# Tap weights through TensorE, one row group of taps and the negated sines on GpSimd, ssm_k first in the queue

## The chip, the core and the metric

The kernel runs on one core of one Trainium2 chip. A core has TensorE (matmuls, into PSUM), VectorE, ScalarE, GpSimd and SyncE, each with its own instruction queue; SyncE and ScalarE also issue loads and stores. The metric is the device time of one execution in microseconds, taken as the median of several runs. The profile calls TensorE PE, its weight loads PEld, VectorE DVE, ScalarE ACT, GpSimd POOL and SyncE SP; a "q" behind a name means the queue that issues, not the engine's own work. L12 is line 12 of the kernel.

## The reference

A block with a long convolution, computed by Fourier transforms, followed by a two-layer network. S is 2048 positions, D is 512 channels. Cut to what matters here:

```python
k_shift = sum(k_pad[:, t:t + S, :] * shift_k[:, ks - 1 - t] for t in range(4))   # four taps a channel
kv = k_shift * v
y = irfft(rfft(pad(kv)) * rfft(pad(ssm_k)))[:S] + kv * ssm_D
h = x + layernorm(x) * y
out = h + relu(layernorm(h) @ w1) @ w2
```

`shift_k` is 512x4 (the tap weights), `ssm_k` 512x2048, `ssm_D` 512; all in bf16.

## The kernel before

The Fourier transforms are done as matmuls with tables of sines in several stages. The whole program is written out in one order by hand; each engine works through its own queue strictly in that order, and semaphores hold it where another engine's result is not there yet.

**Loads at the start.** SyncE's queue issues, in this order: `wsh`, the tap weights as 128 partitions x 4 row groups x 4 taps, which are runs of four bf16 numbers, eight bytes each (L123); `sk`, the 2 MB of ssm_k (L124); then for four chunks `c` of 512 positions the transposed load of k into `kT[c]` (L134, L136) and of v into `vT` (L137). ScalarE's queue issues two small loads of ssm_D (L128). The 512 channels are four "row groups" of 128.

**Zero products.** Until ssm_k has landed, TensorE multiplies zeros: `fill(ps, n)` issues n matmuls of 128x512 whose result nobody reads, 28 at L158.

**Small tables.** GpSimd makes index ramps, the two unit matrices `identw` and `ident` (L178), the large ramp `r2` (L180) and the mask `dmask` (L246). VectorE makes `wf`, the tap weights in float32 (L191), and the angles `t1`, `t3` (helper `_turns`, L44 and L46), the parts `f1hi` and `f1lo` of the first stage's table (L215), and the large angles `tsn` (L222, L220). ScalarE makes sixteen diagonal matrices `wdiag`, `ident` times one column of `wf` each (L204).

**Transposes.** `to_rows` turns ssm_k by 32 matmuls with `identw` (L284) into five PSUM tiles `pst`, which ScalarE (L287) and VectorE (L289) copy out.

**The loop over `gb`, seven groups.** In each group `taps(c, h)` does two row groups of one chunk: four matmuls of 128x512 per row group with `wdiag` (one per tap, L335), and then VectorE multiplies the sum by v in place (L338). So chunk 1, row groups 2 and 3 are done in group 3. Then `stage1` does 32 small matmuls (L300) into two PSUM tiles `ps1`; VectorE adds the mask and copies one half of each (L312), ScalarE copies the other half of each (L315). The copies of one tile wait for each other: ScalarE's second copy comes after VectorE's first, and VectorE's second after ScalarE's first.

**The PSUM ring.** `bank2` hands out four tiles of two banks in a ring. A tile can be written again once the readers of the tile four places earlier are done. A group of the loop takes three: one `pkv` for the taps and two `ps1` for stage1. So the first `ps1` of a group waits for the L338 of the group before, and the second `ps1` for both copies out of the first `ps1` of the group before.

**Sines in the loop.** `st` holds three blocks of 64 columns per row: the sines of `tsn` (one big instruction before the loop, L236), the sines of `r2`, and the negated sines of `tsn`. `more_sines(gb)` behind group gb makes one half of a block on ScalarE (L236): in groups 0 and 1 the negated ones, in groups 2 and 3 those of `r2`. Behind group 1 `ec_turns(0)` lets GpSimd write new angles over the first half of `tsn` (L257, L260), which therefore has to wait until the negated sines have read it. Behind group 3 VectorE wraps these angles (`ec_wrap`, L264), and ScalarE makes four sines of them (`ec_sins`, L268), one behind each of groups 4 and 5 and two inside group 6.

**Then.** GpSimd makes tables for later (L362 to L370) and, once the last of the four sines has been read from the memory that they share, the sum tables `smc` (L377, L383), which the first sums (L459) read at 50.8 us. Behind the loop `vT` is turned (L284), stage1 of group 7 and eight groups of stage1 of `xfl` follow (evictions L273, L275), then the products in the frequency domain, the inverse stages (L584, L675) and the network (L687, L703). None of these is touched.

Of the kernel before, what the change touches and what calls it, by code (L numbers as in the profile page):

```python
# [9 lines left out]
ALU = mybir.AluOpType  # L10
BF16 = mybir.dt.bfloat16
F32 = mybir.dt.float32  # L12
# [3 lines left out]
P = 128  # L16
# [25 lines left out]
def _turns(nc, out, r, col, M, quarter):  # L42

    nc.vector.tensor_scalar(out=out, in0=r, scalar1=col, scalar2=float(M // 2 + (M // 4 if quarter else 0)),  # L44
                            op0=ALU.mult, op1=ALU.add)
    nc.vector.tensor_single_scalar(out=out, in_=out, scalar=M - 1, op=ALU.bitwise_and)  # L46
# [10 lines left out]
def kernel(  # L57
# [13 lines left out]
    nc = tc.nc  # L71
    _, S, D = A_q.shape
    DFF = B_w1.shape[1]
    KS = A_shift_k.shape[1]
    assert S == 2048 and D == 512 and KS == 4, "kernel is specialised to S=2048, D=512, ks=4"
    NT = 16
    DC = D // P
# [7 lines left out]
    consts = pl.push("consts")  # L85
# [5 lines left out]
    early = pl.push("early", side="right")  # L91
# [8 lines left out]
    G = turnp.tile([P, 4096], I32, name="G")  # L100
    taken = [15424]

    def view(at, n, dt, t=E):
        return t[:, at:at + n].bitcast(dt)

    def small(shape, dt):
        n = math.prod(shape) * (2 if dt == BF16 else 4) // 4
        v = view(taken[0], n, dt)
        taken[0] += n
        return v.rearrange("p (a b) -> p a b", a=shape[0]) if len(shape) == 2 else v  # L110

    CH = 512
    sk = view(0, 4096, BF16).rearrange("p (c t) -> p c t", c=DC)
    kfl = view(4096, 4096, BF16).rearrange("p (c n) -> p c n", c=P)
    vT = view(8192, 4096, BF16).rearrange("p (c t) -> p c t", c=DC)
    wdiag = view(12288, 1024, BF16).rearrange("p (r j c) -> p r j c", r=DC, j=KS)
    kT = [view(13312 + 1056 * c, 1056, BF16).rearrange("p (r t) -> p r t", r=DC) for c in range(2)]
    kT += [view(1056 * c, 1056, BF16, F).rearrange("p (r t) -> p r t", r=DC) for c in range(2)]
    r2 = G[:, 0:2048].rearrange("p (a b) -> p a b", a=32)
    tsn = G[:, 2048:4096].rearrange("p (a b) -> p a b", a=32)  # L120

    wsh = consts.tile([P, DC, KS], BF16, name="wsh")
    nc.sync.dma_start(out=wsh[:], in_=A_shift_k.rearrange("(r p) j -> p r j", p=P))  # L123
    nc.sync.dma_start(out=sk, in_=A_ssm_k.rearrange("(c p) t -> p c t", p=P))  # L124
    draw = small([DC * P], BF16)
    for dp in range(2):
        src = bass.AP(tensor=A_ssm_D.tensor, offset=A_ssm_D.offset, ap=[[0, 1], [1, DC * P]])
# [22 lines left out]
    def bank2(name):  # L150
        return psum.tile([P, 2, 512], F32, tag="ps", name=name)[:]

    def fill(ps, n):

        for _ in range(n):
            nc.tensor.matmul(out=ps, lhsT=zero[:], rhs=zero[:].unsqueeze(1).to_broadcast([P, 4, P]), start=True, stop=True, skip_group_check=True)

    fill(bank2("psz")[:, 0, :], 28)  # L158

    n1i = early.tile([P, 1], I32, name="n1i")  # L160
    for s in range(0, P, 32):
# [12 lines left out]
    ident = early.tile([P, P], BF16, name="ident")  # L174
    identw = early.tile([P, P], F32, name="identw")
    for t in (identw, ident):
        nc.gpsimd.memset(t[:], 0.0)
        nc.gpsimd.affine_select(out=t[:], in_=t[:], compare_op=ALU.not_equal, fill=1.0,  # L178
                                base=0, pattern=[[-1, P]], channel_multiplier=1)
    nc.gpsimd.iota(r2, pattern=[[2, 32], [128, 64]], base=1, channel_multiplier=0)  # L180
    pi4 = consts.tile([P, 2], I32, name="pi4")
    nc.gpsimd.iota(pi4[:], pattern=[[0, 2]], base=0, channel_multiplier=1)
# [4 lines left out]
    n2c = consts.tile([P, 1], F32, name="n2c")  # L187
    nc.vector.tensor_copy(out=n1c[:], in_=n1i[:])
    nc.vector.tensor_copy(out=n2c[:], in_=n2i[:])
    wf = early.tile([P, DC, KS], F32, name="wf")  # L190
    nc.vector.tensor_copy(out=wf[:], in_=wsh[:])  # L191
    t1 = small([64], I32)
    _turns(nc, t1[:, 0:32], r1[:], n1c[:], 128, True)
    _turns(nc, t1[:, 32:64], r1[:], n1c[:], 128, False)
    t3 = small([2, 64], I32)
    _turns(nc, t3[:, 0, :], r3[:], n2c[:], 64, True)
    _turns(nc, t3[:, 1, :], r3[:], n2c[:], 64, False)
# [19 lines left out]
    st = stp.tile([P, 32, 192], F32R, name="st")  # L217
# [17 lines left out]
    def big_sin(out, turns, scale):  # L235
        nc.scalar.activation(out=out, in_=turns, func=ACT.Sin, scale=scale * TURN / 8192)  # L236
# [18 lines left out]
    def ec_turns(q):  # L255
        w = ecw[q]
        nc.gpsimd.iota(w[:, 1, :].rearrange("p (i a n) -> p i a n", i=4, a=4), pattern=[[1, 4], [16, 4], [64, 32]],  # L257
                       base=4 * q, channel_multiplier=0)
        for h, off in ((0, 4096 + 2048), (1, 0)):
            nc.gpsimd.tensor_scalar(out=w[:, h, :], in0=w[:, 1, :], scalar1=k1o[:], scalar2=float(off),  # L260
                                    op0=ALU.mult, op1=ALU.add)

    def ec_wrap(q):
        nc.vector.tensor_single_scalar(out=ecw[q], in_=ecw[q], scalar=8191, op=ALU.bitwise_and)  # L264

    def ec_sins(q, rs=range(DC)):
        for r in rs:
            nc.scalar.activation(out=ecore[q][:, :, :, r // 2, r % 2, :], in_=ecw[q].rearrange("p h (i x) -> p h i x", i=4),  # L268
                                 func=ACT.Sin, scale=esc[:, r:r + 1], bias=ebi[:, r:r + 1])
# [22 lines left out]
    def stage1(fl, B, gb, dmul=None):  # L292

        j, sp = gb // 2, gb % 2
        pss = [bank2("ps1").rearrange("p b (a w r l x) -> p (b a) (w r) l x", a=2, w=2, r=2, l=2) for _ in range(2)]
        for gi in range(8):
            g = 16 * j + 4 * (gi // 2) + 2 * sp + gi % 2
            for f, first in ((f1hi, True), (f1lo, False)):
                for rp, rows in enumerate(halves):
                    nc.tensor.matmul(out=pss[rp][:, gi // 2, :, gi % 2, :],  # L300
                                     lhsT=fl[rows, 2 * g:2 * g + 2, :].rearrange("p d n -> p (d n)"),
                                     rhs=f[rows].rearrange("p w r v h -> p (w r v h)"), start=first, stop=not first,
                                     tile_position=(64 * rp, 0), skip_group_check=True)
        o = [B.rearrange("p i (u w) (v s) x -> p i u w v s x", w=2, s=2)[:, :, 4 * j:4 * j + 4, :, :, sp, 4 * rp:4 * rp + 4]
             .rearrange("p i u w v x -> p i (u w) v x") for rp in range(2)]
        pv = [p.rearrange("p u (w r) l (v i) -> p i (u w) v (r l)", w=2, i=2) for p in pss]
        if dmul is None:
            for rp in range(2):
                copy("AD"[rp], o[rp], pv[rp])
            return  # L310
        for rp in range(2):
            nc.vector.tensor_tensor(out=o[rp][:, 0], in0=pv[rp][:, 0],  # L312
                                    in1=dmul[:, rp, sp, 4 * j:4 * j + 4].rearrange("p u w x -> p (u w) x").unsqueeze(2)
                                    .to_broadcast([P, 8, 16, 4]), op=ALU.add)
            nc.scalar.copy(out=o[1 - rp][:, 1], in_=pv[1 - rp][:, 1])  # L315
# [4 lines left out]
    big_sin(st[:, :, 0:64], tsn, 1)  # L320

    def more_sines(i):
        half = slice(16 * (i % 2), 16 * (i % 2) + 16)
        if i < 2:
            big_sin(st[:, half, 128:192], tsn[:, half], -1)
        else:
            big_sin(st[:, half, 64:128], r2[:, half], 1)

    def taps(c, h, each=2):

        for r0 in range(2 * h, 2 * h + 2, each):
            ps = bank2("pkv")[:, 0:each, :]
            for i in range(each):
                for j in range(KS):
                    nc.tensor.matmul(out=ps[:, i, :], lhsT=wdiag[:, r0 + i, j, :],  # L335
                                     rhs=kT[c][:, r0 + i, 16 - j:CH + 16 - j], start=(j == 0), stop=(j == KS - 1))
            vv = vT[:, r0:r0 + each, CH * c:CH * c + CH]
            nc.vector.tensor_tensor(out=vv, in0=ps, in1=vv, op=ALU.mult)  # L338
# [2 lines left out]
    inv3 = consts.tile([P, 2, 2, 64], F32R, name="inv3")  # L341
    inv12 = consts.tile([P, 2, 64], F32R, name="inv12")
    ones = consts.tile([P, P], F32R, name="ones")

    for gb in range(7):
        if gb < 6:
            taps(gb // 2, gb % 2)
        else:
            taps(3, 0)
            taps(3, 1, 1)  # L350
            ec_sins(0, (2, 3))
        stage1(kfl, BK, gb, dmask)
        if gb < 4:
            more_sines(gb)
        if gb == 1:
            ec_turns(0)
        if gb == 3:
            ec_wrap(0)
        if gb in (4, 5):
            ec_sins(0, (gb - 4,))  # L360

    nc.gpsimd.memset(inv3[:].bitcast(F32), 0.0)  # L362
    nc.gpsimd.tensor_tensor(out=dpm[:, 0, :], in0=dsc[:, 0, :], in1=dsc[:, 1, :], op=ALU.add)
# [118 lines left out]
    for c in range(8):  # L482
        units, early = {}, {}
# [43 lines left out]
    st = late.tile([P, 4, 6], F32, name="st")  # L527
# [185 lines left out]
    psz = pl.push("psZ", space=PSUM)  # L713
# [74 lines left out]
```

## Time and profile before

| what | us |
|---|---|
| median of three runs (207.43 to 208.14) | 207.6 |
| the profiled execution | 207.31 |
| its span, first to last instruction | 205.2 |
| TensorE busy | 197.6 |
| VectorE busy | 141.9 |
| ScalarE busy | 116.4 |
| GpSimd busy | 69.4 |

An engine's busy time is the union of its instructions' spans. In a timeline a row gives start, length, engine, line, operation, output<-input with sizes, and how many instructions of one kind are merged in it (x8); in square brackets stands how long the engine sat idle before it and what released it. In the chain of waits, each piece is what the end of the program had to wait for at that moment, with its start and length. A table by stage gives for each stretch its length and then the busy time of PE, PEld, DVE, ACT and POOL with the number of instructions, the granted TensorE clock, the busy share of the DMA engines, and GB/s.

### The profile page before, as it was taken

How to read it: one execution, taken by the hardware profiler on the slowest of the kernel's cores; microseconds unless marked ns; L12 is line 12 of the kernel's file. 1: busy time of each engine (PE TensorE's matmuls, PEld its weight loads, DVE VectorE, ACT ScalarE, POOL GpSimd, SP SyncE). 2: the span in 40 equal slices, each digit the busy share in tenths (PEclk: the TensorE clock that was granted, in tenths of full speed). 3: DMA queues.
4: the chain of work that ended last, by engine and by line, in shares of the span. 5: the costliest groups of instructions: out<-in, count | busy, mean ns of one | idle time of the engine just before them, and what ended most of it. 6: DMA issues, size and time to landing. Idle time of an engine off the chain costs nothing.

```text
span 205.2 us, 4606 instructions
## 1 busy us (share of the span) xinstructions
PE 197.6 (96%) x1869; PEld 138.1 (67%) x1869; DVE 141.9 (69%) x246; ACT 116.4 (57%) x190; POOL 69.4 (34%) x118
## 2 busy tenths in 40 slices
PE   8999999988999999999999999999999999999991
PEld 2475555977899999899998844475444844444460
DVE  5989898699789998997652875998098642360130
ACT  5776779788577877677781088304940164026200
POOL 7962800991467996122003032052102200002000
PEclk9999999999999999999999999999999999999997
DMA  5999980001700000064526999899806805310011
GB/s 151 345 214 196 199 141 3 0 5 16 265 0 3 0 3 3 0 130 78 102 67 194 208 221 144 169 154 136 120 16 126 140 25 52 84 58 13 0 51 51
DMA packets 47819, 19.93 MB, mean 97 GB/s; under 512 B 42710, under 2 KB 46264, under 8 KB 47800
## 3 DMA queue, kind: packets, MB, share of 16 engines
q1 hardware_dynamic: 44144, 16.15, 41.6%
q10 hardware_dynamic: 3656, 3.51, 6.3%
q8 instruction: 14, 0.23, 0.5%
q14 instruction: 5, 0.04, 0.1%
HBM read 7.02 MB, written 2.10 MB: 44 GB/s over the span
## 4 chain that ended last, share of the span: by engine, by line
PE 90%; DMA 4%; ACT 2%; DVE 1%; issue 1%; SPq 0%
PE ps1m L687 19%; PE ps2m L703 19%; PE psi L584 11%; PE us L459 8%; PE ps L300 8%; PE pz L675 7%; PE u L437 7%; PE pkv L335 7%; DMA E<-in_A_ssm_k_dram 4%; PE pst L284 3%; PE pm L507 1%; ACT xfl L287 0%; ACT BX L273 0%; DVE BX L475 0%; DVE BK L312 0%
## 5 line engine op out<-in xcount | busy, mean ns | idle before, releaser
L689 ACT ACTIVATE M<-ps1m 128x512 bf16<-128x512 f32 (+1 forms) x44 | 25.1, 595 | 49.4 <-PE ps1m L687 39.0
L703 PE MATMUL ps2m<-M 128*128 128x512 bf16 (+3 forms) x187 | 38.7, 366 | 0.0
L703 PEld LDWEIGHTS <-M 128*128 128x128 bf16 (+1 forms) x187 | 18.3, 98 | 19.9
L687 PEld LDWEIGHTS <-w 128*128 128x128 bf16 (+1 forms) x176 | 17.4, 100 | 19.9
L383 POOL TENSOR_TENSOR smc<-st 64x256 fp32r<-64x256 f32 x32 | 22.8, 730 | 10.3 <-PE us L459 9.4
L546 POOL TENSOR_SCALAR rstd<-mv 128x4 f32<-128x4 f32 x8 | 2.2, 276 | 70.2 <-DVE mv L544 70.2
L705 DVE SCALAR_TENSOR_TENSOR M<-ps2m,rstd,M 128x512 bf16<-128x512 f32 (+1 forms) x13 | 9.2, 706 | 22.3 <-PE ps2m L703 13.8
L475 DVE TENSOR_TENSOR BK<-u,ktu 128x512 fp32r<-128x512 f32 x32 | 21.2, 685 | 3.5 <-ACT ktu L423 1.9
L584 PE MATMUL psi<-inv,BK 128*128 128x128 f32 x128 | 21.1, 256 | 0.0
L423 ACT COPY ktu<-u 128x512 f32<-128x512 f32 x32 | 17.9, 593 | 5.3 <-PE u L437 4.5
L584 PE MATMUL psi<-inv,BX 128*128 128x256 f32 x64 | 20.4, 337 | 0.0
L584 PEld LDWEIGHTS psi<-inv,BK 128*128 128x128 f32 x128 | 19.7, 197 | 0.0
L687 PE MATMUL ps1m<-M,w 128*128 128x512 bf16 (+1 forms) x88 | 19.3, 379 | 0.0
L687 PE MATMUL ps1m<-xT,w 128*128 128x512 bf16 (+1 forms) x88 | 19.3, 379 | 0.0
L459 PE MATMUL us<-BK,smc 64*128 64x256 f32 x128 | 14.5, 302 | 0.6 <-ACT BX L273 0.6
L437 PE MATMUL u<-BK,st 64*128 64x256 f32 x128 | 13.5, 290 | 0.2 <-DVE BX L475 0.2
L459 PE MATMUL us<-BX,smc 64*128 64x256 f32 x128 | 13.3, 282 | 0.0
L437 PE MATMUL u<-BX,st 64*128 64x256 f32 x128 | 13.0, 281 | 0.0
L584 PEld LDWEIGHTS psi<-inv,BX 128*128 128x128 f32 x64 | 12.1, 196 | 0.3 <-DVE BK L475 0.3
L542 DVE BATCH_NORM_STATS2 st<-M 128x6 f32<-128x512 bf16 x20 | 12.3, 677 | 0.0
L315 ACT CAST BK<-ps 128x512 fp32r<-128x512 f32 x16 | 9.3, 584 | 5.0 <-PE ps L300 3.3
L661 DVE TENSOR_TENSOR qT<-pz,qT 128x2048 bf16<-128x2048 f32 x2 | 4.6, 2292 | 10.1 <-DMA qT<-M 6.0
(126 smaller groups left out, 409.1 us busy)
## 6 DMA issues: line engine op xcount, KB each, us to landing
E<-in_A_ssm_k_dram SPq DMA_DIRECT2D x1, 2048.0 KB
out_dram<-M ACTq DMA_DIRECT2D x15, 128.0 KB
w<-in_B_w_dram SPq DMA_DIRECT2D x1, 1376.0 KB
M<-in_B_w_dram ACTq DMA_DIRECT2D x1, 1280.0 KB
M<-in_A_q_dram SPq DMA_DIRECT2D x8, 128.0 KB
xh<-in_A_q_dram SPq DMA_DIRECT2D x4, 128.0 KB
xr<-in_A_q_dram SPq DMA_DIRECT2D x4, 128.0 KB
out_dram<-M ACTq DMA_DIRECT2D x2, 64.0 KB
```

What stands on the lines that cost most here:

```text
L300: nc.tensor.matmul(out=pss[rp][:, gi // 2, :, gi % 2, :], lhsT=fl[rows, 2 * g:2 * g + 2, :].rearrange("p d n -> p (d n)"), rhs=f[rows].rea ...
L335: nc.tensor.matmul(out=ps[:, i, :], lhsT=wdiag[:, r0 + i, j, :], rhs=kT[c][:, r0 + i, 16 - j:CH + 16 - j], start=(j == 0), stop=(j == KS - 1))
L383: nc.gpsimd.tensor_tensor(out=smc[pq, c % 3, i, :, 64 * dp:64 * dp + 64], in0=st[pq, ks, 64:128].bitcast(F32), in1=st[pq, ks, 0:64].bitcas ...
L423: nc.scalar.copy(out=kt[:], in_=ps)
L437: nc.tensor.matmul(out=ps[:, dp, 256 * x:256 * x + 256], lhsT=t[pq], rhs=cols((BK, BX)[x], pq, k1, i), start=not begun, stop=(i == 1), til ...
L459: mm = nc.tensor.matmul(out=ps[:, k % 2, 256 * x:256 * x + 256], lhsT=smc[pq, k // 4 % 3, i, k % 4, :], rhs=cols((BK, BX)[x], pq, k, i), s ...
L475: nc.vector.tensor_tensor(out=o, in0=ps[:, :, 256:512].rearrange("p b (g x) -> p b g x", x=8), in1=kt[:].rearrange("p b (g x) -> p b g x", ...
L584: nc.tensor.matmul(out=o if part == 0 else o[:, P * part - P:P * part], lhsT=src[:, g // 2, :, g % 2::2].rearrange("p c r -> p (c r)"), rh ...
L675: nc.tensor.matmul(out=pz[:, i, :, a:a + w, :].rearrange("p (s r) a n -> p s r (a n)", s=2), lhsT=ax[rho][:, n2 // 2, n2 % 2, :], rhs=ecor ...
L687: nc.tensor.matmul(out=ps1[:fsz, :].rearrange("p (i t) -> p i t", i=4), lhsT=w1[:, c, fc * P:fc * P + fsz], rhs=hT[sc][:, :, c, :], start= ...
L689: nc.scalar.activation(out=h1T[:fsz, fc, :], in_=ps1[:fsz, :], func=ACT.Relu)
L703: nc.tensor.matmul(out=ps2, lhsT=h1T[:ksz, fc, i * P:(i + 1) * P], rhs=w2[:ksz, fc, d0:d0 + w], start=(fc == 0), stop=(fc == NFC - 1))
```

## The change

It does five things.

- The tap weights are loaded as `wrow`, four partitions with 512 numbers in a row each, by ScalarE's queue ahead of the loads of ssm_D; SyncE's queue begins with ssm_k.
- TensorE turns `wrow` by four products with a 4x4 corner of `ident` into a PSUM tile `psw`, and VectorE's `wf` is a copy of that, moved behind the two `_turns` for `t1`. The zero products become 7 before and 17 behind the turning: 24 instead of 28.
- The negated sines are made by GpSimd from the finished sines, in one instruction of 2048 elements a partition, behind `ec_turns(0)`; both stand ahead of the loop now, since `tsn` is no longer read by the negated sines.
- The taps of chunk 1, row group 3, are computed by GpSimd: four multiplications by a column of `wf`, three additions, and the product with v. Group 3 of the loop does row group 2 only.
- The sines of `r2` are made behind groups 0 and 1, `ec_wrap` follows behind group 1, and the four `ec_sins` behind groups 2 to 5.

```diff
-    wsh = consts.tile([P, DC, KS], BF16, name="wsh")
-    nc.sync.dma_start(out=wsh[:], in_=A_shift_k.rearrange("(r p) j -> p r j", p=P))
+    wrow = small([DC * P], BF16)[0:DC, :]
     nc.sync.dma_start(out=sk, in_=A_ssm_k.rearrange("(c p) t -> p c t", p=P))
+    nc.scalar.dma_start(out=wrow, in_=A_shift_k.rearrange("(r p) j -> r (p j)", p=P))
...
-    fill(bank2("psz")[:, 0, :], 28)
+    fill(bank2("psz")[:, 0, :], 7)
...
+    psw = bank2("psw")[:, 0, 0:KS * DC].rearrange("p (j r) -> p j r", j=KS)
+    for j in range(KS):
+        nc.tensor.matmul(out=psw[:, j, :], lhsT=wrow[:, j::KS], rhs=ident[0:DC, 0:DC], start=True, stop=True, skip_group_check=True)
+    fill(bank2("psz")[:, 0, :], 17)
...
-    wf = early.tile([P, DC, KS], F32, name="wf")
-    nc.vector.tensor_copy(out=wf[:], in_=wsh[:])
     t1 = small([64], I32)
     _turns(nc, t1[:, 0:32], r1[:], n1c[:], 128, True)
     _turns(nc, t1[:, 32:64], r1[:], n1c[:], 128, False)
+    wf = early.tile([P, DC, KS], F32, name="wf")
+    nc.vector.tensor_copy(out=wf[:], in_=psw.rearrange("p j r -> p r j"))
...
     def more_sines(i):
-        half = slice(16 * (i % 2), 16 * (i % 2) + 16)
-        if i < 2:
-            big_sin(st[:, half, 128:192], tsn[:, half], -1)
-        else:
-            big_sin(st[:, half, 64:128], r2[:, half], 1)
-
-    def taps(c, h, each=2):
-
-        for r0 in range(2 * h, 2 * h + 2, each):
+        half = slice(16 * i, 16 * i + 16)
+        big_sin(st[:, half, 64:128], r2[:, half], 1)
+
+    def taps(c, h, each=2, n=2):
+
+        for r0 in range(2 * h, 2 * h + n, each):
...
+    def taps_gpsimd(c, r):
+
+        acc, tap = G[:, 3072:3584].bitcast(F32), G[:, 3584:4096].bitcast(F32)
+        for j in range(KS):
+            nc.gpsimd.tensor_scalar(out=tap if j else acc, in0=kT[c][:, r, 16 - j:CH + 16 - j], scalar1=wf[:, r, j:j + 1],
+                                    scalar2=0.0, op0=ALU.mult, op1=ALU.add)
+            if j:
+                nc.gpsimd.tensor_tensor(out=acc, in0=acc, in1=tap, op=ALU.add)
+        vv = vT[:, r, CH * c:CH * c + CH]
+        nc.gpsimd.tensor_tensor(out=vv, in0=acc, in1=vv, op=ALU.mult)
+
+
+    ec_turns(0)
+    nc.gpsimd.tensor_scalar(out=st[:, :, 128:192], in0=st[:, :, 0:64].bitcast(F32), scalar1=-1.0, scalar2=0.0, op0=ALU.mult, op1=ALU.add)
+    taps_gpsimd(1, 3)
 
     for gb in range(7):
-        if gb < 6:
+        if gb == 3:
+            taps(1, 1, 1, 1)
+        elif gb < 6:
             taps(gb // 2, gb % 2)
         else:
             taps(3, 0)
             taps(3, 1, 1)
-            ec_sins(0, (2, 3))
         stage1(kfl, BK, gb, dmask)
-        if gb < 4:
+        if gb < 2:
             more_sines(gb)
         if gb == 1:
-            ec_turns(0)
-        if gb == 3:
             ec_wrap(0)
-        if gb in (4, 5):
-            ec_sins(0, (gb - 4,))
+        if gb in (2, 3, 4, 5):
+            ec_sins(0, (gb - 2,))
```

## The prediction

> **What bounds the kernel now.** I read the page's chain of waits first, then its pieces in order of time, then busy time by stage.
>
> ```profile
> PE 90%; DMA 4%; ACT 2%; DVE 1%; issue 1%; SPq 0%
> ...
> 1.25 8.16 DMA E<-in_A_ssm_k_dram
> 9.55 4.08 PE pst L284 x32
> 13.63 1.73 PE pkv L335 x8
> ...
> 22.03 1.84 PE pkv L335 x8
> 23.87 1.00 PE ps L300 x32
> ```
>
> ```profile
> 9.50:35.00 25.50, 25.45 (x320) 15.70 (x320) 22.39 (x33) 19.29 (x24) 10.08 (x22) 1.00 0.89 160
> ```
>
> The chain is one load (ssm_k, landed at 9.41) and then TensorE to the end; from 9.5 to 35 us TensorE (first number after the length) is busy 25.45 of 25.50. So two things can shorten the run: an earlier landing, and fewer matmuls before 35 us. But VectorE is busy 22.39 of that 25.50 (fourth number), so its slack is small. One row group's cycle in detail, VectorE and then ScalarE:
>
> ```profile
> 19.38 1.28 DVE L312 TENSOR_TENSOR BK<-ps,dmask 128x512 fp32r<-128x512 f32 x2
> 21.07 1.23 DVE L338 TENSOR_TENSOR E<-pkv,E 128x1024 bf16<-128x1024 f32 x1 [0.42 <-PE pkv L335]
> 22.21 1.28 DVE L312 TENSOR_TENSOR BK<-ps,dmask 128x512 fp32r<-128x512 f32 x2
> ```
>
> ```profile
> 22.93 0.58 ACT L315 CAST BK<-ps 128x512 fp32r<-128x512 f32 x1 [0.24 <-DVE BK L312]
> ```
>
> In a period of 2.84 us VectorE is idle 0.42. The second L315 waits for the first L312 and ends at 23.51. It frees the first `ps1` of this group, and the ring of four PSUM tiles (`pkv`, `ps1`, `ps1` per group) gives that very slot to the second `ps1` of the next group, whose matmuls start at 23.80. That is 0.29 us of slack: a shorter `taps` cannot bring stage1 much forward unless this chain moves too.
>
> **The load first.** SyncE's queue issued the tap weights at 0.72 and ssm_k at 1.25:
>
> ```profile
> 0.72 0.47 SPq L123 DMA_DIRECT2D wsh<-in_A_shift_k_dram  x1
> 1.25 0.49 SPq L124 DMA_DIRECT2D E<-in_A_ssm_k_dram  x1
> ```
>
> ssm_k now goes at 0.72: **-0.53 us**, landing about 8.88. Bounds: 0 (if something later, not the issue, sets the landing) to -0.60 (DMA activity begins at 1.8 us with the tap weights' eight-byte runs, its rate rises at 2.4; those runs no longer stand ahead). I take the issue rows, 0.53. The eight transposed loads behind it go 0.53 sooner too. ScalarE's queue gets one issue more, ahead of the two loads of ssm_D, about 0.5 us; its table load moves from 1.57 to about 2.1 and ends near 3.4, where the first small sine (3.37) waits for VectorE anyway; the first reader of ssm_D is GpSimd at 6.55.
>
> **The weights through TensorE.** From the start of the zero products:
>
> ```profile
> 1.38 1.91 PE L156 MATMUL psz<-zero 128*128 128x512 bf16 x4
> ...
> 7.72 1.46 PE L156 MATMUL psz<-zero 128*128 128x512 bf16 x6
> ```
>
> With one lasting 0.63 early and 0.38 late, the pitch is (1.91-0.63)/3 = 0.427 at first and (1.46-0.38)/5 = 0.216 at the end; it changes near 5.05. Seven from 0.97 end their stream at 3.96, later than `ident` (GpSimd, 3.63). The four turning products have no row; bounds per product 0.06 (the pitch of L300's small ones) to 0.43 (an early zero product); I take 0.15, a weight load at the early clock (98 ns late, 147 early): 0.6, to 4.56. Seventeen zeros: one slow, sixteen at 0.216, end near 8.6, before 8.88. So nothing; at the upper bound 9.5, 0.6 lost. `wf` comes near 4.8 instead of 2.93. The sixteen L204 on ScalarE begin then (were 3.96, 4.77 us in all), end at 9.6, the next sine at 9.9; ScalarE's first eviction is due at 10.72-0.53 = 10.19. Cover 0.3 us, and the slot that the eviction frees at 11.2 is wanted at 12.6, by the twenty-ninth transpose. Behind `wf` in VectorE's queue stand the `t3` turns, but they lose nothing:
>
> ```profile
> 3.61 1.98 DVE L44 TENSOR_SCALAR E<-E,n2c 128x64 int32<-128x64 int32 x1
> 5.73 0.25 DVE L44 TENSOR_SCALAR E<-E,n2c 128x64 int32<-128x64 int32 x1
> ```
>
> ```profile
> 3.60 1.94 POOL L180 IOTA G<- 128x2048 int32 x1
> ```
>
> The same operation took 1.98 us instead of 0.25 because it could not run beside GpSimd's iota and ended just after it (5.59 after 5.54). It will end there again.
>
> **A row group of taps off TensorE.** Four matmuls at 0.216: -0.86 us in group 3. On GpSimd: four scalar multiplies (L260: 0.69 each for 512) and four tensor_tensors (L364: 0.32 for 64, L383: 0.73 for 256, so about 1.28 for 512) make 7.9 us; the negated sines 1.97 (L248, as many elements). GpSimd was idle from 13.8 to 18.87 and from 25.4 to 35.5; its tables for the first sums ended at 47.2; now they follow the last sine (near 32.6) with 2.8 of memsets and 8.9 of L383, to 44.3. L459 reads them at 50.8. The tap products are ready near 27.3, needed at 35. Covered.
>
> **The sines.** ScalarE drops two L236 (1.06 each), the rest move up. Per group it was idle 0.2 to 0.7, so they fit; L315 of group 6 starts 0.18 sooner, but the copy behind it waits for VectorE (35.83) as before: nothing.
>
> **What takes the taps' saving back.** `ec_wrap` (L264, 0.68 long, 0.60 of queue) moves from behind group 3 to behind group 1, just ahead of group 2's L338. I count in the clock of before. The second L312 of group 1 starts at 19.98, so L264 can go at 20.58, L338 of group 2 at 21.18 instead of 21.07, plus any wait w of L264. For w: GpSimd is idle beside L264 now and is not after the change, and by the L44 row such an operation waits out GpSimd's current instruction. Both follow the big sine (13.90+1.93 = 15.83): L264 comes 4.75 after its end. GpSimd starts 0.07 after it and needs until 2.20 for its three `ec_turns` instructions (18.80 to 21.00 now); the negation takes 1.97 to 4.17; the first tap multiply then runs to 4.86. So w = 0.1. Bounds: 0, and 2.05 if the negation runs at tensor_tensor's 2.2 ns an element (4.6 us); nearest is L248, one input and 2048 elements, so 0.1.
>
> [...]
>
> Then L338 starts at 21.28, the first L312 at 22.42 and ends at 23.10, L315 ends at 23.71, TensorE may start group 3's second `ps1` at 23.76. It wanted 23.80-0.86 = 22.94. It waits 0.8 of the 0.86: **-0.05 us** is left. Every further 0.1 us of w costs 0.1.
>
> **Sum.** -0.53-0.05 = -0.58. The profiled execution took 207.31 (span 205.2 and 2.1 around it), so 206.7; the median of the runs is 0.29 above it, so **207.0**. Everything after 35 us follows TensorE and shifts along.
>
> **Rivals.**
> - *The ring does not hold TensorE; the taps' 0.86 comes in full.* For it: in the whole loop now TensorE shows no wait on a PSUM tile. Against it: the slack is 0.29. 207.6-0.53-0.86 = 206.2. Chance 0.24.
> - *Slower: L264 stuck behind GpSimd* in VectorE's queue at group 1, with group 2's L338 behind it and TensorE's next tile behind that. Decides from w = 0.68 (no gain left), and above 1.3 the loss is measurable; at 2.05, 1.4 us lost: 209.0. For it: the negation on float32 rows of 64 has no row. Chance 0.22, of which 0.15 beyond 208.2.
> - *Slower: the clock opens late.* The zero products run slowly for 4.1 us; if the turning products' pause makes that count begin again at 4.56, nine slow and eight fast ones end at 4.56+3.84+1.73+0.16 = 10.3 instead of before 8.88, 1.4 lost: 208.4. The row speaks neither way. Chance 0.10. [...]
> - *The load lands no sooner*: 207.55. For it: the transfer, 6.5 of the 8.16 us, is unchanged. Chance 0.04.
>
> My forecast has 0.40, its own range 206.9 to 207.5 (w from 0 to 0.5).
>
> **How the numbers follow.** 0.3% is 0.62 us, about what a measurement of this kernel tells from no change. Faster: 0.24 and 0.20 of the forecast's 0.40, as 207.0 lies on that edge. Slower: 0.15+0.10. The rest, 0.31, is the same. The range reaches to the full saving below and to the late clock above, 206.1 to 208.6, and leaves out the far end of w.
>
> **What would show it.** First pst matmul near 9.0 instead of 9.55 (load; if 10 or later, the clock). L264's own duration: 0.7 to 0.8, or up to 2.7 (w). A TensorE wait of about 0.8 ahead of group 3's L300 released by ScalarE's L315: with it the taps gave nothing, without it the first rival holds. The negation: 2.0 us. Wrong altogether would be a wait on GpSimd after 35 us, or waits on ScalarE's L204 at the first `pkv`.

## The result, and the profile after

| what | before | after |
|---|---|---|
| median, us (10 runs each, side by side) | 207.51 (207.21 to 208.37) | 206.75 (206.41 to 207.15) |
| ratio, with its 95% interval | | 0.9960 (0.9947 to 0.9973) |
| the profiled execution, its span | 207.31, 205.2 | 206.94, 204.8 |
| TensorE, VectorE, GpSimd busy | 197.6, 141.9, 69.4 | 195.9, 140.8, 79.7 |

The changed kernel is faster by 0.76 us, 0.4%. Lines have moved: the taps' product with v is L340 (was L338), the copies out of `ps1` are L317 on VectorE and L320 on ScalarE (were L312, L315), the stage1 products are L305 (L300), `ec_wrap` is L269 (L264), the turns of ssm_k L289 and their evictions L294 and L292.

First the profile page's chain of waits after, shares of the span by engine:

```profile
PE 88%; DVE 8%; ACT 1%; issue 1%; DVEq 0%
```

Before, the load (4%) and TensorE (90%) were the chain. The load has gone from it, and VectorE has 8% where it had 1%. The same chain in order of time (start, length, what; short pieces are left out) says where:

```profile
0.98 3.16 PE psz L157 x7
4.57 1.02 DVE E L44
8.27 1.35 DVE G L227
9.64 1.23 DVE G L225
11.74 1.13 DVE E L294
13.34 1.46 PE pkv L337 x6
...
20.61 1.22 DVE E L340
21.83 0.61 DVE BK L317
22.46 0.59 ACT BK L320
23.10 1.05 PE ps L305 x31
```

Two stretches are new. Up to 12.9 us the chain runs through VectorE's own queue of table work, whose last eviction (L294, a copy of turned ssm_k out of PSUM) releases the first taps. The seven zeros stand at its head, but it was not they that held VectorE: its L44 behind them ended with GpSimd's iota, as before (5.58 after 5.54 us). At 20 to 23 us it runs through one PSUM tile's copies and on to TensorE. TensorE's timeline shows both, and the start (start, length, line, operation, tile, size, number; in brackets the idle time before and its releaser):

```profile
0.97 3.17 PE L157 MATMUL psz<-zero 128*128 128x512 bf16 x7 [0.97 <-DVE pbias L144]
4.07 0.29 PE L183 MATMUL psw<-ident,E 4*128 4x4 bf16 x4
4.29 4.07 PE L157 MATMUL psz<-zero 128*128 128x512 bf16 x17
8.85 3.85 PE L289 MATMUL pst<-identw,E 128*128 128x128 f32 x32 [0.49 <-DMA E<-in_A_ssm_k_dram]
12.91 1.89 PE L337 MATMUL pkv<-E 128*128 128x512 bf16 x7 [0.21 <-DVE E L294]
...
22.38 0.23 PE L305 MATMUL ps<-f_hi,E 64*128 64x128 bf16 x1
23.10 0.21 PE L305 MATMUL ps<-f_hi,E 64*128 64x128 bf16 x1 [0.49 <-ACT BK L320]
```

The first `pst` is 0.70 earlier than before (9.55), the first `pkv` only 0.56 (13.47 before). In group 3 the second product starts 0.72 behind the first, where 0.055 is the usual distance (the pitch): 0.66 us of the 0.86 that the taps gave up is waited for there. The bracket says 0.49, because the first product's own row, 0.23 long, counts as busy. The chain through `ps1` on VectorE, and the end of the loop:

```profile
4.40 0.17 DVE L199 COPY wf<-psw 128x16 f32<-128x16 f32 x1 [1.05 <-PE psw L183]
4.49 1.09 DVE L44 TENSOR_SCALAR E<-E,n2c 128x64 int32<-128x64 int32 x1
...
17.68 1.22 DVE L340 TENSOR_TENSOR E<-pkv,E 128x1024 bf16<-128x1024 f32 x1 [0.29 <-PE pkv L337]
18.82 1.28 DVE L317 TENSOR_TENSOR BK<-ps,dmask 128x512 fp32r<-128x512 f32 x2
20.02 0.68 DVE L269 TENSOR_SCALAR G<-G 128x1024 int32<-128x1024 int32 x1
20.61 1.22 DVE L340 TENSOR_TENSOR E<-pkv,E 128x1024 bf16<-128x1024 f32 x1
21.75 1.27 DVE L317 TENSOR_TENSOR BK<-ps,dmask 128x512 fp32r<-128x512 f32 x2
...
32.29 2.42 DVE L340 TENSOR_TENSOR E<-pkv,E 128x1024 bf16<-128x1024 f32 x3 [1.01 <-DMA E<-in_A_v_dram]
```

From 17.68 to 21.75 no bracket stands behind a row but the first: VectorE does not stop until the ring has made TensorE wait. The wrap has its own 0.68 and no more. At 32.29 VectorE waits for a transposed load of v, which it did not before; more on that below. GpSimd after:

```profile
3.60 1.94 POOL L185 IOTA G<- 128x2048 int32 x1
...
17.52 1.91 POOL L359 TENSOR_SCALAR st<-st 128x2048 fp32r<-128x2048 f32 x1
19.39 1.86 POOL L350 TENSOR_SCALAR G<-E,wf 128x512 f32<-128x512 bf16 x2
21.34 1.27 POOL L353 TENSOR_TENSOR G<-G 128x512 f32<-128x512 f32 x1
22.71 0.69 POOL L350 TENSOR_SCALAR G<-E,wf 128x512 f32<-128x512 bf16 x1
```

The negation takes 1.91 us. The first two tap multiplies take 1.86 together where one alone takes 0.69: the second started at 20.06, just after the wrap (20.02), and took 1.20. By stage, in the stretch that the prediction showed:

```profile
9.50:35.00 25.50, 24.37 (x311) 14.94 (x314) 22.21 (x34) 18.42 (x24) 22.67 (x33) 1.00 1.01 153
```

TensorE is busy 24.37 us of the 25.50 (25.45 before). Of the 1.13 us in which it is idle, 0.21 lies ahead of the first taps, 0.49 in group 3, and 0.19 ahead of the transposes of v, behind the late load. GpSimd went from 10.08 to 22.67.

### The profile page after: what moved, and what is told of

It reads as the page before. It is cut to its first block, busy times and chain, and to the rows that moved or that the text cites. A ratio compares the mean times of both kernels' runs of the same rounds, so it can differ in the third digit from the quotient of the medians.

```text
span 204.8 us, 4597 instructions
## 1 busy us (share of the span) xinstructions
PE 195.9 (96%) x1857; PEld 137.5 (67%) x1865; DVE 140.8 (69%) x246; ACT 114.8 (56%) x188; POOL 79.7 (39%) x127
## 4 chain that ended last, share of the span: by engine, by line
PE 88%; DVE 8%; ACT 1%; issue 1%; DVEq 0%
PE ps1m L703 19%; PE ps2m L719 18%; PE psi L600 11%; PE us L475 9%; PE pz L691 7%; PE u L453 7%; PE ps L305 7%; PE pkv L337 5%; PE pst L289 2%; PE psz L157 2%; DVE E L340 1%; DVE BK L317 1%; DVE BX L280 1%; DVE G L227 1%; DVE G L225 1%
## 5 line engine op out<-in xcount | busy, mean ns | idle before, releaser
L399 POOL TENSOR_TENSOR smc<-st 64x256 fp32r<-64x256 f32 x32 | 22.9, 733 | 12.9 <-PE us L475 12.1
L320 ACT CAST BK<-ps 128x512 fp32r<-128x512 f32 x16 | 9.4, 586 | 6.9 <-PE ps L305 5.1
```

The lines of the kernel that those rows point to most:

```text
L399: nc.gpsimd.tensor_tensor(out=smc[pq, c % 3, i, :, 64 * dp:64 * dp + 64], in0=st[pq, ks, 64:128].bitcast(F32), in1=st[pq, ks, 0:64].bitcas ...
```

## The experiments

Medians with lowest and highest; each was timed beside the kernel before on one chip, and the ratio to that is given with its 95% interval. Runs e1 to e4, e5 to e8 and e9 to e12 shared a chip each, and are compared with each other inside their group first. In those groups the kernel before took 207.48, 207.35 and 207.44. Each single run also comes with its span, to 0.1 us; run time less span is mostly 2.0 to 2.2 us.

### Which part brings the gain: e1, e2

e1_load_alone is the kernel before with the first two points of the change alone:

```diff
...
+    wrow = small([DC * P], BF16)[0:DC, :]
     nc.sync.dma_start(out=sk, in_=A_ssm_k.rearrange("(c p) t -> p c t", p=P))
+    nc.scalar.dma_start(out=wrow, in_=A_shift_k.rearrange("(r p) j -> r (p j)", p=P))
...
-    fill(bank2("psz")[:, 0, :], 28)
+    fill(bank2("psz")[:, 0, :], 7)
...
+    for j in range(KS):
+        nc.tensor.matmul(out=psw[:, j, :], lhsT=wrow[:, j::KS], rhs=ident[0:DC, 0:DC], start=True, stop=True, skip_group_check=True)
+    fill(bank2("psz")[:, 0, :], 17)
...
+    nc.vector.tensor_copy(out=wf[:], in_=psw.rearrange("p j r -> p r j"))
```

> Load part alone: ssm_k first, tap weights as rows turned by TensorE, 24 zero products; taps, negated sines, wrap and sines as before. Theory (the load is nearly all of the gain): first transpose near 8.85 us instead of 9.55, the first taps matmul 0.5 to 0.6 us sooner because VectorE's eviction of the second PSUM tile stays at 11.65 to 12.86 us; run 0.55 us shorter than before, 206.95 beside 207.5, ratio 0.9974. Rival (the taps on GpSimd bring the gain): no change from before, 207.5.

Measured: 206.62 (206.59 to 206.69), ratio 0.9955 (0.9940 to 0.9971), 0.33 below the expectation. The load's part alone is as fast as the whole change (206.75, timed apart from it). Its chain of waits stands here just ahead of the first taps:

```profile
11.53 0.19 DVE ebi L237
11.72 1.12 DVE E L293
12.85 0.04 issue
12.89 1.89 PE pkv L339 x8
```

The first `pst` was at 8.88, so 0.67 sooner than before, and the first `pkv` at 12.89, 0.58 sooner; here too VectorE's eviction is what releases it. The transposes of v begin 0.58 sooner by the chain of waits (34.53 against 35.11), and the lowest runs of the two kernels lie 0.53 apart (206.59 and 207.12). The rest of the 0.86 between the medians is scatter of the kernel before, which took 207.12 to 208.54 here; e5 comes back to it.

e2_taps_alone is the changed kernel with those two points undone: the load of `wsh` first, 28 zeros, `wf` from `wsh`.

> Taps part alone: GpSimd taps and negated sines, sines and wrap two groups sooner; loads, tap weights and 28 zero products as before. Theory: TensorE waits at group 3 for most of the 0.86 us that it saves, so 0.05 to 0.2 us shorter than before, 207.3 to 207.45, with a wait of 0.5 to 0.8 us ahead of the second PSUM tile of group 3. Rival (the ring does not hold it): 0.86 us shorter, 206.65.

Measured: 207.22 (206.99 to 207.73), ratio 0.9987 (0.9974 to 0.9999): 0.26 us, barely told from nothing. The start of its TensorE timeline:

```profile
0.97 8.80 PE L157 MATMUL psz<-zero 128*128 128x512 bf16 x28 [0.97 <-DVE pbias L144]
9.61 4.01 PE L285 MATMUL pst<-identw,E 128*128 128x128 f32 x32
```

No bracket stands behind `pst`: in this execution the zeros became fast late, and the 28 zeros, not the load, held the transposes. A zero product comes 0.427 us behind the one ahead of it at first and 0.216 later, as the prediction read; the first fast one stood at 6.37 us here and at 5.13 in the profile before. Behind this start, group 3's second product waited 0.52 for ScalarE's copy, and the transposes of v began 0.14 sooner than before (34.97 against 35.11). So the taps' part was held by the ring here as well.

### The rival's mechanism made to happen: e3

The changed kernel with the negation done twice:

```diff
     nc.gpsimd.tensor_scalar(out=st[:, :, 128:192], in0=st[:, :, 0:64].bitcast(F32), scalar1=-1.0, scalar2=0.0, op0=ALU.mult, op1=ALU.add)
+    nc.gpsimd.tensor_scalar(out=st[:, :, 128:192], in0=st[:, :, 0:64].bitcast(F32), scalar1=-1.0, scalar2=0.0, op0=ALU.mult, op1=ALU.add)
```

> The changed kernel with the negation done twice by GpSimd, so that its second 1.9 us lie over the moment at which VectorE comes to the wrap (20.0 us). Theory (wrap waits out GpSimd's instruction, and lateness of VectorE there is paid one for one): the wrap lasts about 1.95 us instead of 0.68, the wait at group 3 grows from 0.5 to about 1.7 us, run 1.2 us longer than the changed kernel: 207.95, ratio to before 1.002. Rival (the PSUM ring has the slack for it, or the two engines do not shut each other out): 206.8, as the changed kernel.

Measured: 207.71 (207.55 to 209.51), ratio 1.0018 (0.9996 to 1.0041). VectorE's row of the wrap, and GpSimd's rows beside it:

```profile
19.98 1.84 DVE L269 TENSOR_SCALAR G<-G 128x1024 int32<-128x1024 int32 x1
```

```profile
17.39 1.91 POOL L359 TENSOR_SCALAR st<-st 128x2048 fp32r<-128x2048 f32 x1
19.38 1.90 POOL L360 TENSOR_SCALAR st<-st 128x2048 fp32r<-128x2048 f32 x1
```

The wrap began inside the second negation, which ends at 21.28, and ended 0.54 after it: 1.84 instead of 0.68, so w = 1.16. The transposes of v began at 35.51 by the chain of waits, against 34.36 in e9 below: 1.15 later. So 1.16 us of w cost 1.15 us, and with it the change's gain is gone. (Two of the twelve runs took 209.19 and 209.51, with spans 1.5 and 1.8 us longer than the median's; they were not traced.) The traces show the two engines holding each other up in both directions: 1.84 instead of 0.68 for the wrap here, which began inside GpSimd's instruction, and 1.20 instead of 0.69 for GpSimd's second multiply in the changed kernel, where the wrap was there first.

### What holds the first taps: e4, e6, e7, e11

In the changed kernel and in e1, VectorE's six small operations (`pi4`, `k1o`, `rof`, `esc`, `ebi`) stand ahead of its evictions of ssm_k. e4_vector_prologue is the changed kernel with them behind:

```diff
     for h in range(4):
         to_rows(sk, h, kfl)
+    for t, sh, op in ((0, 2, ALU.logical_shift_right), (1, 3, ALU.bitwise_and)):
+        nc.vector.tensor_single_scalar(out=pi4[:, t:t + 1], in_=pi4[:, t:t + 1], scalar=sh, op=op)
...
     wrap13(r2)
```

> The changed kernel with VectorE's six small instructions for the later angles (0.87 us, ahead of its first eviction) moved behind the two evictions of the turned ssm_k. Theory (VectorE's work ahead of the transposes holds TensorE 0.2 us at the first taps): the eviction of the second tile starts near 11.0 instead of 11.65 us, TensorE's wait of 0.21 us ahead of the first taps goes, run 0.2 us shorter than the changed kernel, 206.55. Rival (the transposed loads of v set the end of the loop anyway): 206.75, and the wait for the last of them grows by 0.2.

Measured: 206.58 (206.35 to 206.82), ratio 0.9953 (0.9936 to 0.9969). The first `pkv` came at 12.37 instead of 12.91, so VectorE did hold it. The changed kernel was not timed in this group (206.75 and 206.53 elsewhere), so whether the run became shorter is not settled. And the chain of waits shows two waits on ScalarE's copies now, at 17.57 (0.30) as well as at 22.98 (0.40): the small operations, put behind, make the first products with v late, and the ring passes that on.

e7_load_prologue is e1 with four of them behind the evictions and `esc`, `ebi` behind group 1; e11_prologue_again is the same kernel on another chip.

```diff
     for h in range(4):
         to_rows(sk, h, kfl)
+    for t, sh, op in ((0, 2, ALU.logical_shift_right), (1, 3, ALU.bitwise_and)):
+        nc.vector.tensor_single_scalar(out=pi4[:, t:t + 1], in_=pi4[:, t:t + 1], scalar=sh, op=op)
...
     wrap13(r2)
...
+        if gb == 1:
+            for t, v in ((esc, TURN / 8192), (ebi, -0.5 * TURN)):
+                nc.vector.tensor_scalar(out=t[:], in0=rows4[:], scalar1=rof[:], scalar2=v, op0=ALU.is_equal, op1=ALU.mult)
```

> The load part alone, with VectorE's four small instructions for k1o and rof moved behind the two evictions, where VectorE waits 0.37 us for GpSimd, and the two for esc and ebi behind group 1. Theory (VectorE's prologue holds TensorE 0.15 to 0.2 us at the first taps, and there is slack to hide it): that wait goes and no other comes, 0.15 to 0.2 us shorter than the load part alone, 206.45. Rival (the loop's ring takes it back at group 1, as the trace of the prologue experiment shows with all six at one place): 206.6.

> The load part with VectorE's six small instructions moved behind the evictions, once more, beside the load part alone on the same chip. Theory: 0.1 to 0.2 us shorter than that, 206.4, the shortest of all. Rival (the difference was between two chips): the same, 206.6.

Measured: 206.40 (206.26 to 206.95), ratio 0.9939 (0.9918 to 0.9961), and again 206.40 (206.34 to 207.38), ratio 0.9951 (0.9928 to 0.9975). The chain of waits of e7:

```profile
0.72 8.06 DMA E<-in_A_ssm_k_dram
8.78 0.05 issue
8.83 3.86 PE pst L281 x32
12.68 0.21 PE pkv L336
...
17.25 0.16 PE ps L297
...
17.44 1.05 PE ps L297 x31
```

The chain is the load and then TensorE again. Of the 0.37 us that the first `pkv` comes sooner (12.52 against 12.89), 0.24 is lost in group 1, whose stage1 takes 1.31 instead of 1.07. The transposes of v begin at 34.33 in e11 against 34.47 in e10, the same chip's e1. So the traces show 0.14, the medians 0.32. Part of the other 0.18 shows in the single runs: two of e10's six have spans of 204.7 instead of 204.5 and lift its median, and run time less span is 2.0 us in most runs of e7 and e11, 2.1 in those of e1 and in most of e10. Why these differ is open.

e6_load_28_zeros is e1 with 21 zeros behind the turning products instead of 17.

```diff
-    fill(bank2("psz")[:, 0, :], 17)
+    fill(bank2("psz")[:, 0, :], 21)
```

> The load part alone with 7 and 21 zero products, 28 in all as before, instead of 7 and 17. Theory (the zeros are the second bound of the start): they end near 9.5 us, after the load (8.85), the first transpose comes 0.6 us later than in the load part alone, and of the 0.86 us some 0.3 are left: 207.2. Rival (the number of zeros does not matter): 206.62.

Measured: 206.70 (206.60 to 207.37), ratio 0.9962 (0.9945 to 0.9979); the theory had 207.2.

```profile
4.30 4.98 PE L156 MATMUL psz<-zero 128*128 128x512 bf16 x21
9.11 3.75 PE L288 MATMUL pst<-identw,E 128*128 128x128 f32 x32
12.88 1.46 PE L339 MATMUL pkv<-E 128*128 128x512 bf16 x5
```

The zeros held the transposes until 9.11, 0.23 later than in e1, and yet the first `pkv` stood at 12.88 as in e1: VectorE's queue hid the lateness. That is the same hold as in e4, seen from its other side. A kernel without the hold should feel the four zeros, but that was not tried. Three of the twelve runs have spans of 204.9 to 205.3, where those of e1 and e10 are 204.5 to 204.7; they were not traced, so whether the zeros cost something in some executions stays open.

### The number of zeros alone: e5

```diff
-    fill(bank2("psz")[:, 0, :], 28)
+    fill(bank2("psz")[:, 0, :], 24)
```

> The kernel before with 24 zero products instead of 28 and nothing else. Theory (the load part gained 0.86 us where the queue's order explains 0.55; the rest is that 28 zeros outlast the load in some executions, where TensorE's fast clock comes later): 0.2 to 0.3 us shorter in the median, 207.2, and the runs closer together, none above 207.7. Rival (the zeros always end before the load lands, as in the first profile, 9.18 before 9.41): no change, 207.5.

Measured: 207.22 (207.15 to 207.41, 12 runs), the kernel before 207.35 (207.15 to 209.00, 29 runs), ratio 0.9985 (0.9969 to 1.0002).

```profile
0.97 6.77 PE L156 MATMUL psz<-zero 128*128 128x512 bf16 x24 [0.97 <-DVE pbias L143]
9.47 3.39 PE L284 MATMUL pst<-identw,E 128*128 128x128 f32 x28 [1.73 <-DMA E<-in_A_ssm_k_dram]
13.15 0.71 PE L284 MATMUL pst<-identw,E 128*128 128x128 f32 x4 [0.29 <-DVE E L289]
```

Here the first fast product stood at 3.91 us (5.13 in the profile before), and the zeros were done 1.73 before the first transpose. VectorE's queue held the last four transposes (its eviction began at 11.88, against 11.65 in the profile before), and the first `pkv` came at 13.70, 0.23 later than before. The lowest times of both kernels are the same; the runs with 24 zeros lie closer together, as expected, but not for the reason expected. The five runs of the kernel before above 208 have spans of 205.0 and 205.1, where the median is 205.1: their extra 0.9 to 1.8 us lie outside the program's first and last instruction, and the zeros lie inside. The spans of both kernels have the same median, 205.1, and reach to 205.4 and 205.3. So no effect of the four zeros is shown.

### Another place for the wrap: e8

The changed kernel with e7's order of the small operations, and the wrap moved into group 3, where TensorE waits anyway; each of the four sines comes one group later.

```diff
         if gb == 3:
             taps(1, 1, 1, 1)
+            ec_wrap(0)
...
-        if gb == 1:
-            ec_wrap(0)
```

> The changed kernel with the prologue split as in the run before this, and the wrap moved from behind group 1 into group 3, between the half-size product with v and stage1, where VectorE sits idle 0.53 us in the changed kernel; the four sines one group later. Theory (what is left of the taps' saving is lost to the ring wait of 0.49 us, of which the wrap ahead of group 2 makes 0.1): the wait at group 3 is 0.35 to 0.4 us, 0.45 of 0.86 is kept, and with the loop's start 0.2 sooner the run is 0.35 us shorter than the changed kernel: 206.35. Rival (the last transposed load of v sets the loop's end): 206.6, with VectorE waiting for a load in group 6.

Measured: 206.46 (206.34 to 206.73), ratio 0.9945 (0.9926 to 0.9964); e7 beside it took 206.40. VectorE's timeline:

```profile
22.69 0.68 DVE L337 TENSOR_TENSOR E<-pkv,E 128x512 bf16<-128x512 f32 x1
23.29 1.45 DVE L262 TENSOR_SCALAR G<-G 128x1024 int32<-128x1024 int32 x1
24.66 1.27 DVE L310 TENSOR_TENSOR BK<-ps,dmask 128x512 fp32r<-128x512 f32 x2
```

GpSimd's tap work ran from 19.39 to 28.16 in the changed kernel; the wrap, put into that stretch, took 1.45 instead of 0.68, and the copy behind it (24.66) was late: stage1 of group 4 took 1.39 instead of 1.07. Group 3 still waited 0.40. So the taps' part gave nothing on top of e7's order: beside the stall in group 3 there was now one in group 4.

### Both again on one chip, and the ring without GpSimd: e9, e10, e12

e9_changed_again is the changed kernel, e10_load_again is e1. e12_taps_left_out is e1 with `taps(1, 1, 1, 1)` in group 3, and nothing in its place on GpSimd, so row group 3 of chunk 1 stays without its taps; wrap, negated sines and the order of the sines stay as before.

> The changed kernel once more, beside the load part alone on the same chip. Theory (the taps part adds nothing in the median, and the changed kernel's runs lie further apart): 206.7, 0.05 to 0.15 us longer than the load part alone, runs over 0.5 us apart. In its trace the group-3 wait of 0.5 us again; whether the last transposed load of v is late (ready at 32.2 in the first trace) shows whether that is this kernel's or that execution's. Rival (the taps part gains and the other chip hid it): 0.15 us or more shorter than the load part alone.

> The load part alone once more, on the same chip as the other three. Theory: 206.6, runs within 0.2 us, all of the changed kernel's gain. Rival: 206.9, and the taps part makes up the difference.

> The load part alone, with the taps of chunk 1, row group 3, left out altogether (v stays unmultiplied there): four matmuls of 128x512 fewer on TensorE, nothing more on GpSimd, wrap and sines as before. Theory (the PSUM ring takes the taps' saving back, not GpSimd): TensorE waits about 0.4 us at group 3 for the copies out of the first stage1 tile of group 2, about 0.45 of the 0.86 us is kept: 206.2. Rival (GpSimd's work and the wrap ahead of group 2 take it back): no wait at group 3, 0.86 us shorter, 205.75.

| run | median | ratio | first `pkv` of group 4 | transposes of v |
|---|---|---|---|---|
| e10, load alone | 206.72 (206.62 to 206.86) | 0.9960 (0.9940 to 0.9980) | 24.23 | 34.47 |
| e9, the whole change | 206.53 (206.39 to 206.67) | 0.9951 (0.9930 to 0.9971) | 24.05 | 34.29 |
| e12, taps left out | 206.36 (206.31 to 206.89) | 0.9947 (0.9926 to 0.9968) | 23.98 | 34.78 |

The last two columns are starts of the first matmul's own row in the profiled execution; it overlaps the row before it by 0.07, which the chain of waits leaves out. The first `pst` stood at 8.82 to 8.95 and the first `pkv` at 12.88 to 12.90 in all three, so the fourth column compares the taps' part alone: the whole change keeps 0.18 of its 0.86 us, and leaving the work out keeps 0.25. Both expectations missed in part: e9 was to be slower than e10 and was 0.19 faster, as its rival said, and e12 was to keep 0.45. TensorE in group 3 of e12:

```profile
22.37 0.23 PE L304 MATMUL ps<-f_hi,E 64*128 64x128 bf16 x1
22.99 0.21 PE L304 MATMUL ps<-f_hi,E 64*128 64x128 bf16 x1 [0.40 <-ACT BK L319]
```

The second product is 0.62 behind the first, 0.57 more than the pitch, with GpSimd doing none of the taps and no wrap ahead of group 2's products. So it is the ring that takes the saving back; GpSimd's work and the earlier wrap add 0.07 to 0.1.

The profiled execution of e12 (206.89) was the slowest of its six, for the reason that also slowed the first profile of the changed kernel. VectorE at the end of the loop, in e12 and then in e9:

```profile
32.30 2.42 DVE L342 TENSOR_TENSOR E<-pkv,E 128x1024 bf16<-128x1024 f32 x3 [1.13 <-DMA E<-in_A_v_dram]
```

```profile
31.66 2.42 DVE L340 TENSOR_TENSOR E<-pkv,E 128x1024 bf16<-128x1024 f32 x3 [0.42 <-PE pkv L337]
```

In e9 the product waits for TensorE alone, as before the change; in e12 and in the first profile of the changed kernel, for the last transposed load of v. By the chain of waits the transposes of v began at 34.81 there, against 34.36 in e9: 0.45 later, which is all of the difference between the two executions (206.94 and 206.49). As e12 has none of the taps on GpSimd, the lateness does not need them.

## Why the prediction held, and where it did not

The forecast was 207.0, with a range of its own from 206.9 to 207.5; 206.75 and 206.53 were measured, below that range and inside the whole one (206.1 to 208.6). The mechanism of each part was as written; several sizes were not.

- **The load, -0.53: right for the load, and right for the loop only by luck, as two omissions nearly cancel.** In this pair of executions the packets of ssm_k begin at 1.95 instead of 2.42 and end at 8.33 instead of 8.93. All traces together say more than one pair: the last packet ended at 8.68 to 8.93 us in the three with the tap weights first (before, e2, e5) and at 8.16 to 8.50 in the eleven with ssm_k first, 0.47 sooner on the mean. The transfer itself took 6.28 to 6.51 in the three and 5.90 to 6.65 in the eleven, so it was unchanged within its scatter, as the term had it. Yet the first `pst` came 0.70 sooner, outside the bound of 0.60: where the zeros did not hold it, it followed the last packet by 0.62 and 0.68 with the old order and by 0.46 to 0.52 with the new. This part is not explained, and the prediction had no term for it. Against that, "everything shifts along" left out VectorE's queue, which does not wait for the load: its eviction of the second tile began at 11.65 before and at 11.65 after. At the first `pkv` 0.56 was left. e4 and e7 moved that hold and got the first `pkv` at 12.37 and 12.52.
- **The weights through TensorE at no cost: right.** The four turning products took 0.29, not 0.6. `wf` was there at 4.57 (4.8 predicted), the zeros ended at 8.36 (8.6), and the `t3` turns ended at 5.58, just after GpSimd's iota, as written (5.59). What the prediction calls the clock is seen in the rows as the pitch of the zeros alone, 0.427 and then 0.216 us: the granted clock stands at 1.00 from 0 to 9 us, before and after, so what makes the pitch change is not shown. It did not change as late as that rival had it, with the zeros' end at 10.3: the first fast product stood at 4.96 (5.13 before). The latest in the eleven executions with the turning products was e12, with the first fast product at 6.36 and the zeros' end at 9.12; e2, which has no turning products, had 6.37, so the pause is not shown to delay it.
- **The wrap, w = 0.1: the mechanism right, the size 0.** It was to go at 20.58 in the clock of before, which less the 0.56 of the start is 20.02, where it stands. The negation took 1.91 (1.97 predicted). The upper end of the forecast's own range stands on a w of 0.5, which no run shows: the wrap took 0.68 in the changed kernel, so w was 0, and 1.84 in e3, where it was 1.16. As GpSimd was in time, the rival of a wrap stuck behind it did not come; e3 brought it about, and its price was 1.15 us for 1.16 of w, as each 0.1 had been priced.
- **The ring's wait, 0.8 of 0.86: right, 0.14 too large.** It was 0.66 in the changed kernel. Without the wrap the prediction's own numbers give 23.51+0.05-22.94 = 0.62, and e12 shows 0.57. What is left of the taps is 0.18 instead of 0.05. That also refutes the rival that the ring would not hold TensorE.
- **The transposed loads "go 0.53 sooner too": wrong.** The first of v was issued 0.56 sooner (9.25 before, 8.69 after), but the last at 25.32 instead of 24.99 in that execution. Over all traces the last was issued at 24.42 to 24.99 with the tap weights first and at 23.67 to 25.63 with ssm_k first: no sooner, while the loop that needs it comes sooner. It cost 0.45 us in the first profile of the changed kernel, and nothing in e9. The prediction had no term for it, and why the queue does not keep its lead is open.
- **What was to be covered: right.** ScalarE had 0.30 us to spare ahead of its first eviction (0.3 predicted), GpSimd's tap product was ready at 28.16 (27.3 predicted), and its tables for the first sums at 44.26 (44.3 predicted).
- **From the profiled time to the median, +0.29: too large.** Beside the changed kernel and in the three groups, the medians of the kernel before were 207.51, 207.48, 207.35 and 207.44, 0.04 to 0.20 above its profiled 207.31.

The sum by the terms as measured: -0.56 at the first taps and -0.18 at group 4 make -0.74, so 206.57 for the profiled execution where no load is late; e9's profile shows 206.49, and its transposes of v stand 0.75 ahead of before (34.36 against 35.11).

The load's part is nearly all of the gain. The taps' part adds 0.19 us by the medians of e9 and e10, and 0.18 by their traces; e2 has 0.26 by its medians and 0.14 by its trace. Against e1, timed apart from them, the changed kernel's first ten runs were 0.13 slower, with the late load among them: their spans go from 204.3 to 205.0, those of e9 from 204.3 to 204.5. Only one of the ten was traced, so how often the load is late is not known. The lowest time of a kernel that does all the work is that of e7 and e11, 206.40, with the load's part and VectorE's small operations moved. It is 0.13 below the changed kernel on the same chip, whose range overlaps with it.

## What to carry to other kernels

When a load comes earlier, look up every queue that must be ready for it: an engine whose own work does not wait for the load turns the earlier load into waiting, as here, where the first `pst` came 0.70 us sooner and the first `pkv` 0.56. Work taken from TensorE inside this ring of PSUM tiles counted only as far as the copies that free the next tile had slack, 0.29 of 0.86 us: 0.18 was kept with the work on GpSimd (e9) and 0.25 with it left out (e12). Where VectorE and GpSimd keep each other out, as the wrap and the negation did in e3 (1.84 us instead of 0.68), place the short instruction by the end of the long one: here the negation ended 0.6 us ahead of the wrap and cost nothing, and 1.9 us more of it on GpSimd undid the whole gain. And one pair of profiles does not settle a tenth of a microsecond: the same transfer of ssm_k took 5.90 to 6.65 us from one execution to the next.

## What the runs showed of the hardware

- The transposed loads drift from execution to execution: the last issue for v was at 23.67 (e8) to 25.63 us (e12), and its last packet of data ended at 28.3 (e8) to 31.7 (e12), under the same issuing order. In e12 VectorE's product then ran at 32.30, in e9 at 31.66.
- The first zero product at the pitch of 0.216 us instead of 0.427 stood at 3.9 (e5) to 6.4 us (e2, e12) into the span. In the profile before it stood at 5.13, and the 28 zeros ended at 9.18, ahead of the load's landing at 9.41; in e2 the 28 zeros ended at 9.77, and the transposes followed them without a wait for the load.
- The profiled execution of e11 took 207.38 and that of e7 206.40, with the same span, 204.4: about 1 us of difference lay outside the program's first and last instruction. So did that of the kernel before's runs above 208 in the group of e5.
